# ScalarE's order in the first attention sequence: scalings behind the next block's exponentials

## The chip, the core and the metric

The kernel runs on one core of a Trainium2 chip. The metric is device time in microseconds (us). Three runs of the kernel before took 1680.72 to 1680.81 us, median 1680.8. One profiled execution gives the trace that is read here.

## The reference

Causal attention with a learned position bias, then a dense mixture of experts. All inputs and outputs are fp32.

```python
B, H, S, D = 4, 8, 576, 64          # attention
scores = q @ k.T / sqrt(D)
cum = cumsum(maximum(s, 0))
scores = where(causal, -1e9, scores + minimum(-(cum_i - cum_j), 0))
attn = exp(scores - max(scores)); attn = attn / (sum(attn) + 1e-9)
x = (attn @ v) as [2304, 512]        # N tokens, D_model

P = exp(x @ w_gate - max)            # 8 experts
for _ in range(8):                   # balance rows and columns
    P /= P.sum(1) + 1e-9; P /= P.sum(0) + 1e-9; P *= N / E
out = sum over e of P[:, e] * (relu(x @ w1[e]) @ w2[e])     # F = 1024
```

## The kernel before, in words

Each fp32 operand of a large product is split into a high and a low part, and three products of parts stand for one. Later stages use a scheme with seven products in place of eight for each 2x2 group of blocks. Those stages take most of the span and are not touched here.

The attention is done per head pair. There are 16 pairs, four per sequence; the first sequence is pairs 0 to 3, called pair 1 to pair 4 in this text. A pair has 576 query rows in five blocks of 128, 128, 128, 128 and 64 rows. Because of the causal mask block i needs only (i + 1) * 128 key columns, so the blocks have 128, 256, 384, 512 and 576 columns. The first four blocks are done for two heads each, on two score banks; in the fifth both heads share one tile of 128 rows, and it is computed in two halves of 288 columns. A block is named by its columns below. One block passes through these steps:

- TensorE computes the scores (tile sc, L605 in the first sequence, L587 later) in a ring of three PSUM banks.
- VectorE forms the row minimum (tile mn, L617) of the negated, masked scores and writes them to an SBUF tile T. There are seven T buffers.
- ScalarE takes the exponential (L652) in place and adds up each row (tile sm).
- VectorE adds 1e-9 to the sums (L703) and takes their reciprocal (tile rec, L709).
- ScalarE multiplies the tile by the reciprocal (L712): the scaling.
- TensorE transposes the tile (tr, L721), VectorE copies the transposes to SBUF (at, L726; for the fifth block al, L729 and L732), and TensorE multiplies them with v (pv, L751). ScalarE and VectorE take the high and low part of that as x (xh, L767 and L768).

Beside this GpSimd prepares the operands of later pairs (L492 to L503 and L556 to L563: casts and subtractions) and, with ScalarE, splits expert weights (L110, L111). A stream of matmuls of the first expert (L149, L178) and of the gate (L776) is given out between the attention blocks as x becomes ready, so TensorE has other work from the second half of the first sequence on.

The loop over the 80 blocks writes down, for step ti, the scores to exponentials of block ti, the sums to scaling of block ti - 1 (st1), the products with v of block ti - 3 and the transposes of block ti - 2. This is the order of the program text. The order on each engine is then set by a scheduler which takes a ready instruction for an engine that its own timeline has free, in program order where several are ready. `tc.issue_after(x)` adds that an instruction stands behind x. Once the order is fixed, each engine works through its own list strictly in turn.

Of the kernel before, what the change touches and what calls it, by code (L numbers as in the profile page):

```python
# [10 lines left out]
AF = mybir.ActivationFunctionType  # L11
# [34 lines left out]
def fused_kernel(ctx: ExitStack, tc: tile.TileContext, qT, kT, v, s, w_gate, wu, out):  # L46
    nc = tc.nc
# [282 lines left out]
    NP0 = 4  # L330
# [327 lines left out]
    last_exp = [None]  # L658
# [34 lines left out]
    def heads(t):  # L693
        return range(2 if t[1] < 4 else 1)

    def st1(t):

        g, i = t
        sm = sums.pop(t)
        nh = len(heads(t))  # L700
        n = (i + 1) * P if i < 4 else S
        if g < NP0:
            nc.vector.tensor_scalar_add(sm[:, :nh], sm[:, :nh], 1e-9)  # L703
        else:
            nc.scalar.activation(
                sm[:, :nh], sm[:, :nh], AF.Identity, bias=guard[:, 0:1], scale=1.0
            )
        rec = apool.tile([P, 2], F32, name="rec", tag="rec", bufs=2)
        nc.vector.reciprocal(out=rec[:, :nh], in_=sm[:, :nh])  # L709
        for j in heads(t):  # L710
            T = Ts[t, j][:, :n]
            nc.scalar.activation(T, T, AF.Copy, scale=rec[:, j : j + 1])  # L712

    def st2(t, j):

# [152 lines left out]
    for ti in range(NS + 3):  # L868
        if ti < NS:
            g, i = slots[ti]  # L870
# [7 lines left out]
        if 1 <= ti <= NS:  # L878
            st1(slots[ti - 1])
# [677 lines left out]
```

## Time and profile before

| | |
|---|---|
| runs (3), median | 1680.8 us (1680.72 to 1680.81) |
| profiled execution | 1679.26 us |
| its span | 1677.5 us, so 1.76 us lie around it |
| TensorE (PE) busy | 1657.0 us, 99% of the span |
| VectorE (DVE) busy | 1171.5 us, 70% |
| ScalarE (ACT) busy | 827.7 us, 49% |
| GpSimd (POOL) busy | 870.0 us, 52% |

Busy times count an engine as busy from the start to the end of an instruction; instructions of one engine overlap by up to a tenth of a microsecond where they follow each other. The idle time that a row gives in brackets is that of the engine just before the instruction, with the instruction that ended it. The clock in the view of stages is the one granted to TensorE, as a share of the full 2.4 GHz.

### The profile page before, as it was taken

The numbers are of one execution on the slowest core, as the hardware profiler recorded it, in microseconds if no ns is written. First come the engines' busy times: TensorE is split into PE (matmuls) and PEld (weight loads), VectorE is DVE, ScalarE is ACT, GpSimd is POOL, SyncE is SP. The second block draws the span as 40 slices with busy tenths as digits, with TensorE's granted clock in tenths as the row PEclk, the third lists the DMA queues.
The fourth block names the chain that finished last, engine by engine and source line by source line (L and its number), as shares of the span: only waits on it lengthen the run. The fifth ranks groups of instructions, "written<-read, shape, count | busy, mean of one in ns | idle before, by whom it ended". The sixth has DMA issues, their size and how long they took to land.

```text
span 1677.5 us, 31297 instructions
## 1 busy us (share of the span) xinstructions
PE 1657.0 (99%) x11213; PEld 1560.9 (93%) x11213; DVE 1171.5 (70%) x2310; ACT 827.7 (49%) x1792; POOL 870.0 (52%) x822
## 2 busy tenths in 40 slices
PE   8999999999999999999999999999999999999999
PEld 6798988888899999999899999999999999999998
DVE  7667666665776776676457777777777777777666
ACT  6777667434544444444235444444445444444443
POOL 7757877433554454454214554545554555455444
PEclk9999999999999999999999999999999999999999
DMA  7647766294975866875956566665688656566552
GB/s 208 176 131 230 212 186 186 92 354 136 316 241 198 276 235 200 279 240 185 354 176 204 182 193 186 187 187 177 204 305 260 193 186 191 182 192 186 187 184 89
DMA packets 202731, 347.54 MB, mean 207 GB/s; under 512 B 20592, under 2 KB 102512, under 8 KB 202512
## 3 DMA queue, kind: packets, MB, share of 16 engines
q1 hardware_dynamic: 202416, 345.23, 64.1%
q8 instruction: 89, 1.46, 0.3%
q14 instruction: 66, 0.54, 0.1%
q10 hardware_dynamic: 160, 0.31, 0.0%
HBM read 246.53 MB, written 94.96 MB: 204 GB/s over the span
## 4 chain that ended last, share of the span: by engine, by line
PE 91%; DVE 4%; ACT 2%; issue 1%; DMA 1%; POOL 0%; SPq 0%; ACTq 0%; DVEq 0%; POOLq 0%
PE c L1193 34%; PE zz L1314 13%; PE zz L1371 13%; PE y L1371 10%; PE g L149 4%; PE g L178 4%; PE sc L587 3%; PE pv L751 2%; PE tr L721 2%; PE c L149 2%; PE c L178 1%; DVE s L1168 1%; ACT T L712 1%; ACT T L652 1%; DVE h L253 1%
## 5 line engine op out<-in xcount | busy, mean ns | idle before, releaser
L253 POOL TENSOR_TENSOR w2o<-r,w2o 128x512 fp32r<-128x512 f32 x192 | 276.5, 1461 | 279.7 <-ACT w2o L1351 271.1
L1371 PE MATMUL zz<-w2o,h 128*128 128x256 f32 x2016 | 272.9, 280 | 0.0
L1193 PE MATMUL c<-xS,w1o 128*128 128x384 f32 x1344 | 271.6, 336 | 1.0 <-ACT t L1208 0.6
L1371 PEld LDWEIGHTS zz<-w2o,h 128*128 128x128 f32 x2016 | 263.3, 188 | 0.3 <-DVE h L253 0.2
L1314 PE MATMUL zz<-w2p,h 128*128 128x512 f32 x1008 | 256.8, 391 | 0.4 <-ACT h L1156 0.4
L1157 DVE SCALAR_TENSOR_TENSOR h<-z,h 128x384 fp32r<-128x384 f32 x252 | 192.7, 770 | 66.2 <-ACT h L1156 63.5
L1156 ACT ACTIVATE h<-z 128x384 fp32r<-128x384 f32 x252 | 130.6, 525 | 207.4 <-DVE z L256 203.5
L1193 PEld LDWEIGHTS c<-xS,w1o 128*128 128x128 f32 x1344 | 227.4, 188 | 2.5 <-DVE z L256 1.2
L1168 DVE SCALAR_TENSOR_TENSOR s<-z,s 128x384 f32<-128x384 f32 x224 | 182.0, 850 | 65.4 <-ACT s L1231 62.4
L253 POOL TENSOR_TENSOR h<-s,h 128x384 fp32r<-128x384 f32 x112 | 137.7, 1237 | 163.2 <-ACT h L1164 162.5
L1314 PEld LDWEIGHTS zz<-w2p,h 128*128 128x128 f32 x1008 | 186.9, 188 | 29.5 <-ACT h L1156 0.7
L1193 PE MATMUL c<-x,w1o 128*128 128x384 f32 x1008 | 203.0, 336 | 0.0
L1371 PE MATMUL y<-w2o,h 128*128 128x256 f32 x1512 | 201.6, 280 | 0.4 <-DVE a L1297 0.3
L1371 PEld LDWEIGHTS y<-w2o,h 128*128 128x128 f32 x1512 | 194.6, 188 | 1.0 <-DVE a L1297 0.5
L256 DVE TENSOR_TENSOR z<-c,t 128x384 f32<-128x384 f32 x252 | 136.7, 550 | 69.8 <-PE c L1193 65.0
L1193 PEld LDWEIGHTS c<-x,w1o 128*128 128x128 f32 x1008 | 170.5, 188 | 0.6
L1297 DVE SCALAR_TENSOR_TENSOR a<-zz,prob,a 128x256 f32<-128x256 f32 (+1 forms) x210 | 110.6, 530 | 67.6 <-PE zz L1371 52.9
L1164 ACT CAST h<-s 128x384 fp32r<-128x384 f32 x224 | 111.0, 513 | 75.7 <-DVE s L1168 70.7
L1193 PE MATMUL c<-xS,wp 128*128 128x384 f32 x672 | 134.5, 336 | 1.3 <-DVE z L256 1.3
L1193 PEld LDWEIGHTS c<-xS,wp 128*128 128x128 f32 x672 | 119.0, 188 | 9.6 <-DVE z L256 2.6
L1351 ACT CAST w2o<-r 128x1024 fp32r<-128x1024 f32 x98 | 102.5, 1047 | 50.9 <-PE y L1371 38.2
L253 POOL TENSOR_TENSOR wp<-s,wp 128x512 fp32r<-128x512 f32 x56 | 80.1, 1430 | 82.8 <-ACT wp L1083 69.7
(166 smaller groups left out, 2638.7 us busy)
## 6 DMA issues: line engine op xcount, KB each, us to landing
w1o<-w1d SPq DMA_DIRECT2D x392, 256.0 KB
w1d<-wp SPq DMA_DIRECT2D x84, 512.0 KB
r<-wu SPq DMA_DIRECT2D x70, 512.0 KB
r<-w2d SPq DMA_DIRECT2D x56, 512.0 KB
sa<-wu SPq DMA_DIRECT2D x28, 512.0 KB
w2d<-sb SPq DMA_DIRECT2D x56, 256.0 KB
wraw<-wu SPq DMA_DIRECT2D x20, 512.0 KB
xS<-xd_S SPq DMA_DIRECT2D x12, 768.0 KB
```

The costliest lines, as they stand in the source:

```text
L149: nc.tensor.matmul(ps[:, :n], lhsT=w1[:, w, o : o + P], rhs=xcols(b, x, k, n0, n), start=(k == 0 and t == 0), stop=(k == KD - 1 and t == 2),)
L253: (eng or nc.gpsimd).tensor_tensor(out=out, in0=a, in1=b, op=ALU.subtract)
L256: (eng or nc.gpsimd).tensor_tensor(out=out, in0=a, in1=b, op=ALU.add)
L1156: mark["a"] = nc.scalar.activation(t[:, 0], z, AF.Relu)
L1157: mark["v"] = nc.vector.scalar_tensor_tensor(out=t[:, 1], in0=z, scalar=0.0, in1=t[:, 0].bitcast(F32), op0=ALU.max, op1=ALU.subtract,)
L1164: nc.scalar.copy(t[:, 0], z)
L1168: nc.vector.scalar_tensor_tensor(out=out, in0=z, scalar=0.0, in1=other, op0=ALU.max, op1=op)
L1193: mm = nc.tensor.matmul(ps, lhsT=w[:, wl, k], rhs=x[:, xl, k], start=(fresh and k == 0 and t == 0), stop=(k == 1 and t == 2), skip_group_c ...
L1297: nc.vector.scalar_tensor_tensor(out=a, in0=ps, scalar=prob[:, c, e : e + 1], in1=a, op0=ALU.mult, op1=ALU.add)
L1314: mm = nc.tensor.matmul(zb[ci], lhsT=h[:, a, ci * P : (ci + 1) * P], rhs=w[:, b_], start=(ui == 0 and f == 0 and t == 0), stop=(ui == UPE ...
L1351: nc.scalar.copy(w[:, :, 0], r)
L1371: nc.tensor.matmul(ps, lhsT=h[:, a, ci * P : (ci + 1) * P], rhs=w[:, ui, b_], start=(fresh and ui == 0 and t == 0), stop=(ui == UPE - 1 an ...
```

## The change

In the first sequence (g below NP0 = 4, the first four pairs) each scaling is issued behind `last_exp[0]`, the last exponential written down so far. When step ti writes the scalings of block ti - 1, that is the last exponential of block ti. Outside the first sequence the line is as before. The three new lines shift what follows, so L712 before is L715 after.

```diff
         for j in heads(t):
             T = Ts[t, j][:, :n]
-            nc.scalar.activation(T, T, AF.Copy, scale=rec[:, j : j + 1])
+            with ExitStack() as st:
+                if g < NP0:
+                    st.enter_context(tc.issue_after(last_exp[0].ins))
+                nc.scalar.activation(T, T, AF.Copy, scale=rec[:, j : j + 1])
```

The first place is ScalarE's list at the start of pair 1, up to the first block of pair 2. L652 is the exponential of a block, L712 its scaling, and x2 stands for two heads. Before:

```order
L652 ACTIVATE T,sm<-T,mn 128x128 x2
L712 ACTIVATE T<-T,rec 128x128 x2
L652 ACTIVATE T,sm<-T,mn 128x256 x2
L712 ACTIVATE T<-T,rec 128x256 x2
L652 ACTIVATE T,sm<-T,mn 128x384 x2
L712 ACTIVATE T<-T,rec 128x384 x2
L652 ACTIVATE T,sm<-T,mn 128x512 x2
L712 ACTIVATE T<-T,rec 128x512 x2
L652 ACTIVATE T,sm<-T,mn 128x576
L767 CAST xh<-pv 128x256
L712 ACTIVATE T<-T,rec 128x576
L652 ACTIVATE T,sm<-T,mn 128x128 x2
```

And the same place now:

```order
L652 ACTIVATE T,sm<-T,mn 128x128 x2
L652 ACTIVATE T,sm<-T,mn 128x256 x2
L715 ACTIVATE T<-T,rec 128x128 x2
L652 ACTIVATE T,sm<-T,mn 128x384 x2
L715 ACTIVATE T<-T,rec 128x256 x2
L652 ACTIVATE T,sm<-T,mn 128x512 x2
L715 ACTIVATE T<-T,rec 128x384 x2
L652 ACTIVATE T,sm<-T,mn 128x576
L715 ACTIVATE T<-T,rec 128x512 x2
L770 CAST xh<-pv 128x256
L652 ACTIVATE T,sm<-T,mn 128x128 x2
L715 ACTIVATE T<-T,rec 128x576
```

Each scaling has moved behind the next block's exponentials. VectorE's list up to the first half of the 576 block is the same before and after.

The second place is VectorE's list from the end of pair 1 to the 256 block of pair 2. L617 is a row minimum (in two rows, the second reads out the minimum), L726 a copy of transposes. Before:

```order
L726 COPY at<-tr 128x384 x2
L703 TENSOR_SCALAR sm<-sm 128x1
L768 TENSOR_TENSOR xh<-pv,xh 128x256
L709 RECIPROCAL rec<-sm 128x1
L617 ISA T,mn<-sc,mask 128x128
L617 ISA mn 128x1
L617 ISA T,mn<-sc,mask 128x128
L617 ISA mn 128x1
L726 COPY at<-tr 128x512 x2
L617 ISA T,mn<-sc,mask 128x256
```

And now:

```order
L703 TENSOR_SCALAR sm<-sm 128x1
L729 COPY at<-tr 128x384
L709 RECIPROCAL rec<-sm 128x1
L729 COPY at<-tr 128x384
L617 ISA T,mn<-sc,mask 128x128
L617 ISA mn 128x1
L617 ISA T,mn<-sc,mask 128x128
L617 ISA mn 128x1
L771 TENSOR_TENSOR xh<-pv,xh 128x256
L729 COPY at<-tr 128x512 x2
L703 TENSOR_SCALAR sm<-sm 128x2
L617 ISA T,mn<-sc,mask 128x256
```

The lone addition of the 576 block has moved ahead of the 384 copies, and the addition of pair 2's first block ahead of the 256 minimum.

The third place is VectorE's list in pair 4, around the minima of the 384 block. Before:

```order
L768 TENSOR_TENSOR xh<-pv,xh 128x256
L703 TENSOR_SCALAR sm<-sm 128x2
L617 ISA T,mn<-sc,mask 128x384
L617 ISA mn 128x1
L617 ISA T,mn<-sc,mask 128x384
L617 ISA mn 128x1
L709 RECIPROCAL rec<-sm 128x2
L729 COPY al<-tr 128x512
```

And now:

```order
L617 ISA T,mn<-sc,mask 128x384
L617 ISA mn 128x1
L617 ISA T,mn<-sc,mask 128x384
L617 ISA mn 128x1
L732 COPY al<-tr 128x512
L703 TENSOR_SCALAR sm<-sm 128x2
L735 COPY al<-tr 128x128
L709 RECIPROCAL rec<-sm 128x2
```

The addition of the 256 block stood ahead of the 384 minima and now stands behind them and behind a copy.

## Rows read from the trace of the kernel before

**Rows 1.** Busy time by stage: stretch and length; busy time and instructions by engine; clock, DMA.
```profile
10.26:17.19 6.93, 4.08 (x31) 2.93 (x32) 4.07 (x19) 4.66 (x16) 5.87 (x11) 0.97 0.91 259
17.19:24.79 7.60, 6.97 (x55) 5.24 (x53) 6.34 (x24) 6.31 (x16) 5.07 (x9) 0.80 0.72 215
24.79:37.87 13.08, 12.16 (x131) 9.31 (x130) 9.88 (x43) 10.58 (x32) 6.87 (x9) 1.00 0.88 235
37.87:50.22 12.35, 11.52 (x119) 8.75 (x121) 9.16 (x41) 10.63 (x31) 9.86 (x19) 1.00 0.54 162
50.22:61.79 11.57, 9.32 (x102) 6.97 (x103) 10.09 (x31) 9.55 (x27) 10.93 (x15) 1.00 0.57 158
...
80.00:260.00 180.00, 180.00 (x1500) 161.17 (x1499) 119.94 (x389) 126.95 (x360) 132.77 (x178) 1.00 0.66 194
```

**Rows 2.** Waits, 10 to 62 us: who waited for whom, total, times, longest.
```profile
DVE sm L703 <- ACT T L652: 9.1, 10, 1.6
...
PE sc L605 <- DVE mn L617: 4.8, 5, 1.9
```

**Rows 3.** Timeline of ScalarE, pair 1: start, length, instruction, shapes, count, idle before.
```profile
11.66 0.69 ACT L712 ACTIVATE T<-T,rec 128x128 f32<-128x128 f32 x2 [0.52 <-DVE rec L709]
12.26 0.49 ACT L652 ACTIVATE T<-T,mn 128x256 f32<-128x256 f32 x1
...
15.57 0.60 ACT L652 ACTIVATE T<-T,mn 128x384 f32<-128x384 f32 x1
```

**Rows 4.** Timeline of VectorE, pair 1.
```profile
11.48 0.40 DVE L617 CUSTOM_DVE_ANT_0 T<-sc,mask 128x256 f32<-128x256 f32 x1
...
13.37 1.10 DVE L703 TENSOR_SCALAR sm<-sm 128x2 f32<-128x2 f32 x1 [1.13 <-ACT T L652]
...
14.58 0.54 DVE L617 CUSTOM_DVE_ANT_0 T<-sc,mask 128x384 f32<-128x384 f32 x1
...
16.90 0.17 DVE L703 TENSOR_SCALAR sm<-sm 128x2 f32<-128x2 f32 x1 [0.89 <-ACT T L652]
...
17.19 0.67 DVE L617 CUSTOM_DVE_ANT_0 T<-sc,mask 128x512 f32<-128x512 f32 x1
...
19.93 0.17 DVE L703 TENSOR_SCALAR sm<-sm 128x2 f32<-128x2 f32 x1 [0.41 <-ACT T L652]
```

**Rows 5.** All additions of L703: duration in ns, least, median, most.
```profile
L703 DVE TENSOR_SCALAR sm<-sm x20: 144/169/1211, 11.2 to 63.2; 128x2 f32<-128x2 f32 x16, 128x1 f32<-128x1 f32 x4
```

**Rows 6.** Timeline of GpSimd, pair 1.
```profile
13.18 1.92 POOL L497 TENSOR_TENSOR ops<-rawq,ops 128x512 fp32r<-128x512 f32 x3
15.18 1.43 POOL L503 TENSOR_TENSOR ops<-rawk,ops 128x576 fp32r<-128x576 f32 x1
...
19.45 1.08 POOL L494 CAST ops<-rawq 128x512 fp32r<-128x512 f32 x3
20.61 1.95 POOL L497 TENSOR_TENSOR ops<-rawq,ops 128x512 fp32r<-128x512 f32 x3
```

**Rows 7.** Timeline of TensorE, the scores of pair 1's 512 block.
```profile
15.18 2.02 PE L605 MATMUL sc<-ops 64*128 64x512 f32 x12 [1.90 <-DVE mn L617]
```

**Rows 8.** Timeline of VectorE, from pair 1 to pair 2.
```profile
23.59 1.28 DVE L726 COPY at<-tr 128x512 f32<-128x512 f32 x2
24.79 0.41 DVE L617 CUSTOM_DVE_ANT_0 T<-sc,mask 128x256 f32<-128x256 f32 x1
```

**Rows 9.** Timeline of VectorE, pair 2.
```profile
29.32 0.37 DVE L703 TENSOR_SCALAR sm<-sm 128x2 f32<-128x2 f32 x1 [1.61 <-ACT T L652]
```

**Rows 10.** Timeline of GpSimd, one subtraction in pair 2, one in pair 4.
```profile
28.38 1.28 POOL L111 TENSOR_TENSOR w<-wraw,w 128x512 fp32r<-128x512 f32 x1
...
53.08 1.41 POOL L559 TENSOR_TENSOR ops<-rx,ops 64x576 fp32r<-64x576 f32 x1
```

**Rows 11.** Timeline of VectorE, pair 4.
```profile
53.30 1.21 DVE L703 TENSOR_SCALAR sm<-sm 128x2 f32<-128x2 f32 x1
54.42 0.54 DVE L617 CUSTOM_DVE_ANT_0 T<-sc,mask 128x384 f32<-128x384 f32 x1
```

## The prediction

> **What bounds the kernel now.** I read the busy time of each engine by stage first [rows 1]. From 80 to 260 us TensorE is busy for all 180.00 us: there the span can only follow TensorE. The first sequence is different. I cut it where VectorE starts the row minima of a head pair's 256-column block: 24.79, 37.87, 50.22, and at 61.79 the last block of the fourth pair. In the five stretches up to there TensorE is busy 4.08 of 6.93, 6.97 of 7.60, 12.16 of 13.08, 11.52 of 12.35 and 9.32 of 11.57 us, so it idles 2.85 + 0.63 + 0.92 + 0.83 + 2.25 = 7.48 us. That idle time is all that the change can win, because the matmuls stay the same and what follows is packed. No other engine is full either: VectorE idles 11.99 of the five stretches' 51.53 us, ScalarE 9.80.
>
> The view of waits says why [rows 2]. VectorE's addition of 1e-9 to the sums (sm, L703) waits 9.1 us for ScalarE's exponential, and TensorE's scores wait 4.8 us for VectorE's row minimum, since a score bank is free only when the minimum has read it. So the three engines hand one block round in a ring: scores, minimum, exponential, sum and reciprocal, scaling, transposes.
>
> **The change part by part.** Nothing is added or removed: 36 scalings (four pairs, each with 4 blocks of two heads and one block of one) go behind the next block's exponentials. No DMA moves on ScalarE's queue; SyncE's list is shuffled by a few places, and its loads have tens of microseconds in hand. In the ring the scaling stood between two exponentials; now the exponential waits only for its own minimum, and the scaling runs while VectorE makes that.
>
> *Pair 1, worked through.* ScalarE has done the first block's exponentials at 11.14 and then idles 0.52 us for the reciprocal before the scalings of 11.66 [rows 3]; the 256 exponentials start behind these, at 12.26. The 256-column minimum of head 0 starts at 11.48 [rows 4] and takes 0.40, so in the new order they can start at about 11.93. The addition behind them starts at 13.37, so they took some 1.07; now they end at about 13.00, and the addition can start at 13.03.
>
> That 0.34 us may be worth more. The addition lasted 1.10 us at 13.37 and only 0.17 at 16.90 [rows 4]; the median of all 20 is 0.169, the longest 1.211 [rows 5]. GpSimd's three subtractions run from 13.18 for 1.92 us, and the first, of 512 columns, is the long one [rows 6]: the addition started inside it and ended, at 14.47, about with it. All six long additions of the sequence lie so. The one at 19.93 took 0.17 although GpSimd was casting (19.45 to 20.53): there a cast held nothing. An addition at 13.03 is ahead of 13.18, so it should take 0.17: the reciprocal and then the 384-column minimum start at about 13.32 instead of 14.58, the scores of block 4 at 13.92 instead of 15.18 [rows 7], and TensorE's wait of 1.90 shrinks by about 1.2.
>
> The next addition loses this. The 384 exponentials now start with their minimum, at about 13.89, and take the 1.30 that lie between 15.57 [rows 3] and the end that the addition of 16.90 waits for [rows 4]: that addition now comes at 15.22. GpSimd's next subtraction runs from 15.18 for 1.43 [rows 6], so I take the addition as held until 16.63, and the 512 minimum starts at 16.74 instead of 17.19: 0.45 is left. The margin is 0.04 us, so this is open (below).
>
> The Trainium skill, "SBUF — State Buffer", section "Who interferes with whom", says that VectorE and GpSimd share a port pair and that whoever issues first has it for the whole instruction, tensor_scalar being one of the kinds that take it. The rows agree for subtractions (a hold of 0.93 at 13.37) and not for casts. By that rule alone, with casts holding too, the cast block from 12.02 would also catch the addition at 13.03, pair 1 would gain nothing, and the sum below would be 1.46.
>
> From the 512 minimum to the next pair's 256 minimum took 17.19 to 24.79, 7.60 us, with VectorE busy for 6.34 [rows 1, 8]. In the new order one more addition stands in front of that minimum, the copy pair of 1.28 us (23.59) still does, and the lone addition of the 576 block comes near 20.8, inside the subtractions that begin at 20.61 [rows 6]. I take 7.7 us. So of 0.45 stay 0.34: the 256 minimum of pair 2 at 24.45. This is the main reason why I expect little: VectorE's copies fill what ScalarE gives up.
>
> *Pair 2.* VectorE idled 1.61 us up to 29.32 for the 384 exponentials, which stood behind the scalings of two blocks, and was then held 0.37 by the subtraction that began at 28.38 [rows 9, 10]. With these scalings moved, the exponentials start right behind their minimum; with the 0.34 carried on I put that at 26.9 and their end, 1.30 later, at 28.2, just ahead of 28.38. The upper end is the idle time and the hold less a normal addition, 1.61 + 0.20 = 1.81; the lower is nothing, where the subtraction wins and the addition ends at 29.69 as now. Also, the exponential of the 576 block now stands behind two scalings. I take a third, 0.63, nearer to the lower end, because that is what the row itself shows.
>
> *Pairs 3 and 4.* In pair 3 the copies stand ahead of the minima in the new order as in pair 2; bounds -0.8 to +0.83 (its TensorE idle time, and as much lost), and I take 0. In pair 4 the addition of 53.30 was held 1.21 us, and the 384 minima stood behind it, at 54.42 [rows 11]; TensorE's scores waited for them. In the new order both minima stand ahead of that addition. This frees at most 54.42 - 53.30 = 1.12; the hold now delays a scaling, which has slack. I take three quarters, 0.83, as later additions can be caught again; bounds -1.4 to 1.12.
>
> *Sum.* 0.34 + 0.63 + 0 + 0.83 = 1.80 us earlier at the end of the sequence, or 24% of the idle 7.48. Behind it the engines' lists are reshuffled on TensorE up to about its thousandth instruction of 10706 and on GpSimd and SyncE somewhat longer, then they agree; TensorE stays packed there, so the 1.80 should pass through. Scalings and transposes that come later are covered by the three other blocks in flight (seven T buffers); if that cover failed it would cost a scaling pair per block, 0.69 for the smallest [rows 3]. The profiled execution took 1679.26 (span 1677.5 and 1.76 around it), 1.54 below the median of 1680.8. Against its own time this gives 1677.46; against the median 1679.0.
>
> **The rivals.**
>
> *A, the additions slip ahead of GpSimd.* If the addition at 15.22 gets in before the subtraction, pair 1 gains 16.63 - 15.39 = 1.24 more, TensorE's granted clock, 0.80 on average from 17.19 to 24.79 after the idle stretch, need not fall, and pair 4 can recover 1.8 of its 2.25 idle. Sum 0.34 + 1.24 + 0.63 + 1.8 = 4.0: 1676.8. For it: the margin is 0.04 us and ScalarE's chain is truly shorter. Against it: VectorE's full list behind it.
>
> *B, VectorE takes the bound.* It is busy in 6.34 of 7.60 us from 17.19 on and in 10.09 of 11.57 in pair 4; the copies and holds eat what ScalarE gives. Then the only gain is about 0.3: 1680.5.
>
> *C, more holds: slower.* The change moves every addition against GpSimd's subtractions, and in pair 4 GpSimd is busy for 10.93 of 11.57 us [rows 1]. One newly caught addition costs up to 1.28 (the subtraction at 28.38) or 1.41 (the one at 53.08) [rows 10]. Three more that each wait in full, one in pair 2 and two in pair 4, cost 1.28 + 1.41 + 1.41 = 4.10, less the 1.80: 2.3 slower, 1683.1. It decides from 1.8 us of new holds on. Against it: six of 20 are held already, and moving an addition can free it as well.
>
> That the change doesn't do what it says is no rival: ScalarE's list shows the swap from the first block on. Only the last block of pair 4 has nothing to wait for but its own exponential.
>
> **How the numbers follow.** Forecast (gain 1.8, its own range 1677.6 to 1680.4): 0.40. A: 0.22. B: 0.23. C: 0.15. A measurement of this kernel tells about 0.2%, 3.4 us, from no change. Faster than 1677.4 is most of A and the edge of the forecast: 0.24. Slower than 1684.2 is half of C: 0.08. Within: 0.68. The range takes A and most of C in: 1675.7 to 1682.8.
>
> **What would show it.** In the changed profile: exponentials of the 256 block at about 11.9; the addition behind them 0.17 long; the third addition held by the subtraction of 15.18; the 256 minimum of pair 2 near 24.45, of pair 3 near 36.9; the 384 minima of pair 4 more than 1 us earlier against that pair's start; TensorE's idle time over the first 62 us down by about 1.8; and TensorE full from 80 us on. I am wrong if the long additions sum to much more or less than now, if TensorE is idle behind 80 us, or if the 256 minimum of pair 2 comes before 23.5.

## The result, and the profile after

The changed kernel takes 1689.9 us (median of 6 runs, 1688.9 to 1693.7) where the kernel before, run beside it, takes 1681.2 (1680.7 to 1682.6). The ratio is 1.0054, with a 95% interval of 1.0043 to 1.0065. So it is 8.7 us slower, where I had forecast 1.8 us faster, and it lies above the range. The profiled execution took 1690.09 us with a span of 1688.3. TensorE is busy for 1661.9 us of it (before: 1657.0) and so idles 26.4 us (before: 20.5). The 4.9 and the 5.9 add up to the 10.8 by which the span grew. The matmuls are the same ones and the mean granted clock fell from 0.999 to 0.995, so I put the 4.9 down to matmuls at a lower clock.

The view of stages says where. The columns are those of [rows 1]: stretch and length, busy time and instructions of TensorE, its weight loads, VectorE, ScalarE and GpSimd, then clock and DMA. This is after; it begins with the stretches of [rows 1]:

```profile
10.26:17.19 6.93, 5.29 (x31) 3.70 (x32) 4.78 (x19) 4.50 (x16) 5.88 (x11) 0.76 0.92 264
17.19:24.79 7.60, 6.04 (x58) 4.71 (x58) 6.63 (x29) 6.63 (x17) 5.06 (x9) 0.99 0.71 202
24.79:37.87 13.08, 12.29 (x134) 9.81 (x134) 10.78 (x43) 10.29 (x31) 6.27 (x8) 1.00 0.84 223
37.87:50.22 12.35, 10.76 (x121) 8.29 (x120) 10.05 (x41) 9.99 (x29) 10.46 (x20) 1.00 0.59 183
50.22:61.79 11.57, 7.95 (x92) 6.41 (x90) 10.37 (x23) 8.84 (x26) 11.34 (x16) 1.00 0.70 197
61.79:80.00 18.21, 16.13 (x126) 14.14 (x127) 12.26 (x44) 11.20 (x36) 5.02 (x7) 0.72 0.40 118
...
160.00:200.00 40.00, 35.74 (x292) 30.57 (x292) 24.04 (x71) 23.02 (x65) 27.13 (x38) 0.96 0.64 191
```

and the same view of before, for the two stretches that [rows 1] did not hold:

```profile
61.79:80.00 18.21, 16.77 (x151) 13.71 (x152) 10.51 (x41) 11.01 (x37) 9.17 (x14) 1.00 0.66 189
...
160.00:200.00 40.00, 40.00 (x331) 35.56 (x331) 24.92 (x81) 29.56 (x83) 35.67 (x52) 1.00 0.71 211
```

Two parts lose. From 50 to 80 us TensorE idles and then works at a granted clock of 0.72; from 160 to 200 us, where it had no gap at all, it idles 4.26 us.

**Up to 57 us TensorE gets ahead as forecast, though not term by term.** VectorE after, the starts of pairs 1 to 4, against [rows 1, 4, 8, 11]:

```profile
13.06 0.17 DVE L703 TENSOR_SCALAR sm<-sm 128x2 f32<-128x2 f32 x1 [0.82 <-ACT T L652]
...
13.35 0.54 DVE L617 CUSTOM_DVE_ANT_0 T<-sc,mask 128x384 f32<-128x384 f32 x1
...
15.27 1.37 DVE L703 TENSOR_SCALAR sm<-sm 128x2 f32<-128x2 f32 x1 [0.50 <-ACT T L652]
...
16.76 0.67 DVE L617 CUSTOM_DVE_ANT_0 T<-sc,mask 128x512 f32<-128x512 f32 x1
...
24.07 0.42 DVE L617 CUSTOM_DVE_ANT_0 T<-sc,mask 128x256 f32<-128x256 f32 x1
...
36.70 0.72 DVE L703 TENSOR_SCALAR sm<-sm 128x2 f32<-128x2 f32 x1
37.34 0.41 DVE L617 CUSTOM_DVE_ANT_0 T<-sc,mask 128x256 f32<-128x256 f32 x1
...
49.71 0.42 DVE L617 CUSTOM_DVE_ANT_0 T<-sc,mask 128x256 f32<-128x256 f32 x1 [0.64 <-PE sc L605]
...
52.14 0.55 DVE L617 CUSTOM_DVE_ANT_0 T<-sc,mask 128x384 f32<-128x384 f32 x1
```

I had put the addition at 13.03 and unheld, the 384 minimum at 13.32, the next addition at 15.22 and held, the 512 minimum at 16.74, pair 2 at 24.45. The 256 minima of pairs 2, 3 and 4 start 0.72, 0.53 and 0.51 us earlier than before, where the terms added up to 0.34, 0.97 and 0.97. So pair 1 gave twice its term, and pair 2 lost 0.19 in place of gaining 0.63: the minimum of 37.34 stands behind the addition of 36.70, which was held. The 384 minima of pair 4 start at 52.14 (before: 54.42), a gain of 1.77 within that pair, where its term was 0.83. The product with v of pair 3's last block starts at 54.77, where before it stood at 56.99: TensorE is 2.2 us ahead.

**Then one addition stands still for 5 us.** VectorE after, pair 4's 512 block, and what GpSimd does meanwhile:

```profile
57.83 5.06 DVE L703 TENSOR_SCALAR sm<-sm 128x2 f32<-128x2 f32 x1 [1.20 <-ACT T L652]
```

```profile
57.34 1.41 POOL L559 TENSOR_TENSOR ops<-rx,ops 64x576 fp32r<-64x576 f32 x1
58.71 1.25 POOL L111 TENSOR_TENSOR w<-wraw,w 128x512 fp32r<-128x512 f32 x1
59.91 0.14 POOL L542 MEMSET ops<- 128x64 f32 x1
...
60.26 0.65 POOL L556 CAST ops<-rawq 128x576 fp32r<-128x576 f32 x1
60.86 0.66 POOL L557 CAST ops<-rawk 128x576 fp32r<-128x576 f32 x1
61.48 0.78 POOL L556 CAST ops<-rawq 128x512 fp32r<-128x512 f32 x2
62.21 0.66 POOL L557 CAST ops<-rawk 128x576 fp32r<-128x576 f32 x1
62.95 1.40 POOL L563 TENSOR_TENSOR ops<-rawq,ops 64x576 fp32r<-64x576 f32 x1
```

Every GpSimd instruction starts some 0.03 to 0.06 us before the last one ends, until the cast of 62.21 ends at 62.87 and the next starts at 62.95. The addition ends in that gap, at 62.89; it met one GpSimd instruction and stood through ten more. The copies that TensorE waits for stand behind it on VectorE, so TensorE has nothing to do, and its clock falls:

```profile
57.95 0.22 PE L587 MATMUL sc<-ops 128*128 128x128 f32 x1
63.43 0.66 PE L724 MATMUL tr<-ident,T 128*128 128x128 f32 x2 [5.26 <-DVE at L729]
```

In stretches of two microseconds the granted clock is 1.00 up to 60, then 0.92, and 0.50 from 62 to 70: 1.2 in place of 2.4 GHz. All additions of L703 after, against [rows 5]:

```profile
L703 DVE TENSOR_SCALAR sm<-sm x20: 144/256/5061, 11.0 to 65.8; 128x2 f32<-128x2 f32 x16, 128x1 f32<-128x1 f32 x4
```

**The second loss** ends in two waits of TensorE:

```profile
169.64 0.50 PE L587 MATMUL sc<-ops 128*128 128x256 f32 x2 [2.80 <-DVE mn L617]
...
197.07 0.74 PE L587 MATMUL sc<-ops 128*128 128x256 f32 x4 [0.71 <-DVE mn L617]
```

That minimum stood on VectorE behind a cast of head operands (L557), which waited for its load in the first case and was held by GpSimd in the second:

```profile
168.49 0.60 DVE L557 CAST ops<-rawk 128x576 fp32r<-128x576 f32 x1 [4.55 <-DMA rawk<-kT]
...
192.62 3.96 DVE L557 CAST ops<-rawk 128x576 fp32r<-128x576 f32 x1
```

Why the load is late stands in SyncE's list. First before, then after; the columns are start, length, instruction and count:

```profile
152.48 0.59 SPq L96 DMA_DIRECT2D xd<-xh  x1
153.17 1.21 SPq L363 DMA_DIRECT2D rawk<-kT  x2
154.47 1.22 SPq L363 DMA_DIRECT2D rawq<-qT  x2
155.78 1.19 SPq L363 DMA_DIRECT2D rawk<-kT  x2
```

```profile
158.72 0.59 SPq L96 DMA_DIRECT2D xd<-xh  x1
159.41 1.21 SPq L363 DMA_DIRECT2D rawk<-kT  x2
161.91 0.56 SPq L268 DMA_DIRECT2D sx<-xd  x1
162.56 2.18 SPq L363 DMA_DIRECT2D rawq<-qT  x2
164.83 1.19 SPq L363 DMA_DIRECT2D rawk<-kT  x2
```

After, a load of x for the next stage (L268) has come in front of the next head's loads. It reads what the store of 158.72 (L96) writes, so the whole queue stands from 160.62 to 161.91 until that has landed. The last loads start 9.05 us later than before, while TensorE was 4.4 us late (product with v of the pair at hand: 155.59 before, 159.95 after). Of the 9.05 the queue had 6.24 already when that store started (158.72 against 152.48); the other 2.81 come behind it. Why it was 6.24 late and not 4.4 stays open.

### The profile page after: what moved, and what is told of

The parts are those of the page before. It is cut to its first block, busy times and chain, and to the rows that moved or that the text cites. A ratio compares the mean times of both kernels' runs of the same rounds, so it can differ in the third digit from the quotient of the medians.

```text
span 1688.3 us, 31292 instructions
## 1 busy us (share of the span) xinstructions
PE 1661.9 (98%) x11213; PEld 1566.0 (93%) x11213; DVE 1180.6 (70%) x2310; ACT 826.4 (49%) x1792; POOL 871.1 (52%) x822
## 4 chain that ended last, share of the span: by engine, by line
PE 89%; DVE 4%; POOL 2%; issue 1%; DMA 1%; ACT 1%; SPq 1%; ACTq 0%; DVEq 0%; POOLq 0%
PE c L1196 34%; PE zz L1317 13%; PE zz L1374 13%; PE y L1374 10%; PE g L149 4%; PE g L178 4%; PE sc L587 2%; PE pv L754 2%; PE tr L724 2%; PE c L149 2%; PE c L178 1%; DVE s L1171 1%; DMA wraw<-wu 1%; DVE h L253 1%; DVE T L617 0%
```

## The experiments

Three theories stood at the start. H: the held addition and what it hands on is all of the loss. H+Q: the hold is one cause, SyncE's reordered list a second. S: the later scalings are at fault, and the hold fills a time that would be idle anyway. Seven kernels were run. Gains are given by the third column, the median less that of the kernel before, run beside it. "Lost to the clock" is the mean span times one minus the mean granted clock, both over all runs of the row (6 to 29): the work that TensorE would have done in that time at the full clock. "Rest" is the mean span without it. The record gives a run's clock to three digits, and one unit of the third is 1.7 us of the span; by the scatter of the runs both columns are uncertain by some half a microsecond.

| kernel | median us | less before beside it | ratio to before, interval | mean span | lost to the clock | rest |
|---|---|---|---|---|---|---|
| before (beside 1 to 4) | 1681.0 | | | 1679.4 | 4.6 | 1674.8 |
| after | 1689.9 | +8.7 | 1.0054 (1.0043 to 1.0065) | 1688.5 | 10.4 | 1678.1 |
| 1: after, other addition | 1681.0 | 0.0 | 0.9998 (0.9989 to 1.0008) | 1679.7 | 5.7 | 1673.9 |
| 2: after, loads first | 1686.5 | +5.4 | 1.0031 (1.0020 to 1.0043) | 1684.0 | 8.4 | 1675.6 |
| 3: after, both | 1676.9 | -4.2 | 0.9977 (0.9967 to 0.9987) | 1675.2 | 4.0 | 1671.3 |
| 4: after, pair 4 split | 1684.6 | +3.6 | 1.0015 (1.0006 to 1.0025) | 1682.2 | 6.6 | 1675.7 |
| 5: before, other addition | 1676.0 | -5.4 | 0.9971 (0.9960 to 0.9981) | 1674.4 | 2.2 | 1672.2 |
| 6: before, loads first | 1681.7 | +0.3 | 1.0005 (0.9996 to 1.0014) | 1680.1 | 4.0 | 1676.1 |
| 7: after, no addition, loads first | 1678.6 | -2.7 | 0.9983 (0.9973 to 0.9992) | 1676.4 | 4.7 | 1671.6 |

**1. Another instruction for the addition.**

```diff
-            nc.vector.tensor_scalar_add(sm[:, :nh], sm[:, :nh], 1e-9)
+            nc.vector.tensor_reduce(
+                out=sm[:, :nh], in_=sm[:, :nh].unsqueeze(2), axis=AX.X, op=ALU.add
+            )
```

> The changed kernel with one thing replaced: the addition of 1e-9 to the sums (line 703, first sequence, 20 instructions of VectorE) becomes a sum over an axis of length 1, so the 1e-9 is left out; every engine's list is otherwise that of the changed kernel, instruction for instruction. Theory H (the hold is the cause, all of it): VectorE's addition for pair 4's last block was held 5.06 us behind GpSimd, and the 11 us follow from that one wait, the half-speed matmuls behind it and the lateness that it hands on. Then no instruction of that line is held, the gap on TensorE at 58 to 63 us and the half clock after it go, and the time is 1677 to 1680 us. Theory H+Q (two causes): the hold costs what is lost up to 93 us, some 4 to 6 us counted from where the kernel stood just before, and the second loss at 158 to 200 us comes from SyncE's reordered list, in which a load that waits for a store to land stands ahead of the loads of heads; then it is 1682 to 1686 us, and TensorE still idles some 4 us between 160 and 200 us. Theory S (the rival: the later scalings are themselves the cause, the hold only fills an idle time that was there anyway): 1688 to 1691 us.

It is 8.7 us faster than the changed kernel, and S falls. No instruction of the line is held any more; one of them starts at 55.83, inside the subtraction of 55.53:

```profile
L703 DVE TENSOR_REDUCE sm<-sm x20: 143/154/156, 11.0 to 59.0; 128x2 f32<-128x2 f32 x16, 128x1 f32<-128x1 f32 x4
```

```profile
55.83 0.15 DVE L703 TENSOR_REDUCE sm<-sm 128x2 f32<-128x2 f32 x1 [1.70 <-ACT T L652]
```

```profile
55.53 1.40 POOL L559 TENSOR_TENSOR ops<-rx,ops 64x576 fp32r<-64x576 f32 x1
```

The Trainium skill, "SBUF — State Buffer", section "Who interferes with whom", says that a tensor_reduce never contends with GpSimd on trn2; these 20 rows agree. The second loss is still there, which speaks for H+Q against H, though 1681.0 lies 1 us under the 1682 to 1686 of H+Q and 1 above the range of H, and TensorE idles 2.5 us between 160 and 200 us where H+Q said some 4:

```profile
161.36 0.73 PE L587 MATMUL sc<-ops 128*128 128x256 f32 x2 [2.21 <-DVE mn L617]
```

**2. The head loads first.** In the loads of x (L268):

```diff
                 for i, o in enumerate(XRAW):
-                    nc.sync.dma_start(out=xs[a][:, i], in_=xd[p, o][:, :, k, ts])
+                    with ExitStack() as st:
+                        if (p, a, o) == (0, 3, "22"):
+                            st.enter_context(tc.issue_after(heads_in[0].ins))
+                        nc.sync.dma_start(out=xs[a][:, i], in_=xd[p, o][:, :, k, ts])
```

> The changed kernel with one edge more: of the stage loads sx<-xd (line 268) one, the fourth job's block 22, is ordered behind the head loads before it, so that on SyncE's list the next head's four loads (rawq, rawk) stand ahead of that load, which waits for a store to land. TensorE, VectorE and ScalarE keep their lists; some GpSimd work moves too. Theory H: the head loads had slack that the first loss used up, the second loss stays at least in part, 1687 to 1690 us. Theory H+Q: the gaps of TensorE between 165 and 175 us (some 3.2 us) and the half-speed matmuls around them go, and the time is 1684 to 1687 us, with the 5.06 us hold still there. Theory S: as before this edit, 1688 to 1691 us.

3.3 us faster than the changed kernel, and in the range of H+Q. Below, lines behind the edit count three on. The queue no longer stands, and TensorE's wait shrinks from 2.80 to 1.17; that of 0.71 near 197 us is gone, because GpSimd's list changed there too and the cast is no longer held. So the gain is not that of the loads' order alone. The 5.06 us hold is still there, now 5.07.

```profile
159.29 1.21 SPq L366 DMA_DIRECT2D rawk<-kT  x2
160.59 1.19 SPq L366 DMA_DIRECT2D rawq<-qT  x2
161.87 2.14 SPq L366 DMA_DIRECT2D rawk<-kT  x2
```

```profile
167.65 0.50 PE L590 MATMUL sc<-ops 128*128 128x256 f32 x2 [1.17 <-DVE mn L620]
```

**3. Both edits.**

> Both edits: no addition on line 703 that GpSimd can hold (the 1e-9 left out), and the head loads ahead of the waiting stage load. Theory H: the same as the first edit alone, 1677 to 1680 us. Theory H+Q: 3 to 5 us faster than the first edit alone, 1677 to 1680 us. Theory S: 1685 to 1691 us.

4.2 us faster than the first edit alone and 12.9 faster than the changed kernel; the two gains apart are 8.7 and 3.3. H predicted no difference between 1 and 3 and falls. The two gains add up within the noise of a microsecond. Of the second loss this wait is the longest that is left:

```profile
159.80 0.50 PE L590 MATMUL sc<-ops 128*128 128x256 f32 x2 [0.67 <-DVE mn L620]
```

**4. Only pair 4's additions in another form.**

```diff
-            nc.vector.tensor_scalar_add(sm[:, :nh], sm[:, :nh], 1e-9)
+            for j in ([slice(0, nh)] if g < 3 else [slice(j, j + 1) for j in range(nh)]):
+                nc.vector.tensor_scalar_add(sm[:, j], sm[:, j], 1e-9)
```

> The changed kernel, but only pair 4's additions are split, each 128x2 addition into two of 128x1 (nothing is left out; pairs 1 to 3 keep theirs; the lists are otherwise the same). In the trace no 128x1 addition of that line was ever held. Theory H and H+Q, if the form of the instruction decides whether it is held: as the first edit, 1677 to 1680 us by H, 1682 to 1686 us by H+Q. If instead any addition that comes at that moment is held, the 5 us wait at 58 us is back in one of the halves, and the time stays at 1688 to 1691 us. Theory S: 1688 to 1691 us.

5.1 us faster than the changed kernel, in the range of H+Q. None of pair 4's nine additions is held, though eight of them start inside a subtraction of GpSimd. That of 57.46 lies in the middle of one:

```profile
57.46 0.15 DVE L704 TENSOR_SCALAR sm<-sm 128x1 f32<-128x1 f32 x1 [0.55 <-ACT T L652]
```

```profile
56.91 1.29 POOL L111 TENSOR_TENSOR w<-wraw,w 128x512 fp32r<-128x512 f32 x1
```

So by the medians 5.1 of the 8.7 us are pair 4's and 3.6 those of the ordinary holds in pairs 1 to 3 (by the mean spans 6.3 and 2.5). Here the form of the same addition decides whether it is held at all.

**5. The first edit in the kernel before** (the same diff).

> The kernel before with the same replacement as the first experiment (the additions of line 703 of the first sequence as a sum over an axis of length 1, the 1e-9 left out; all lists otherwise those of the kernel before). It tells how much of the 4.2 us by which both edits together are below the kernel before (1676.9 against 1681.0) comes from the additions alone, and how much from the later scalings. By the lengthened additions in the trace of before (1.10, 0.37, 0.88, 1.21, 0.76 and 0.35 us, six, against 0.17 unheld) at most 3.6 us can come back, and only what lies on the path. Theory A (the later scalings are worth what the prediction said, 1.8 us, once nothing is held): 1678.5 to 1679.5 us. Theory B (the later scalings are worth nothing, all of the 4.2 us is the additions'): 1676.5 to 1677.5 us. Theory C (before, the holds lie beside other waits): 1680.5 to 1681.5 us, and then the later scalings alone are worth some 4 us.

This I had not expected: 1676.0 us, below all three ranges, and nearest to B. The held additions of the kernel before cost it 5.4 us, more than the 3.65 by which its six long ones exceed 0.17, and no stretch of this profiled execution has a clock below 1.00. But those six are one sample. The two profiled executions are 3.3 us apart (1679.26 and 1675.98), which the 3.65 cover. In the profiled execution of experiment 6, where VectorE's list is that of before, and GpSimd's too up to 200 us, eight additions are long (0.35, 1.10, 0.68, 1.16, 1.22, 1.21, 0.75 and 0.36 us), 5.5 us above 0.17 in all. So what is held changes from one execution to the next. Against experiment 3 the moved scalings show no gain: 1676.0 without them and 1676.9 with them, and the two intervals to before overlap widely.

**6. The second edit in the kernel before** (the same diff).

> The kernel before with the one edge of the second experiment (the fourth job's load of block 22 behind the head loads before it); TensorE, VectorE and ScalarE keep their lists. If the edge only repairs what the change's reordering of SyncE's list broke, it does nothing here: TensorE has no idle time between 160 and 200 us in the trace of before, 1680 to 1682 us. If loads in that order are worth something in any kernel: 1676 to 1679 us.

1681.7 against 1681.3 beside it: nothing. The edge only mends what the change's new order broke.

**7. No addition.** The 20 additions go; the rest as in 3.

```diff
-        if g < NP0:
-            nc.vector.tensor_scalar_add(sm[:, :nh], sm[:, :nh], 1e-9)
-        else:
+        if g >= NP0:
```

> The changed kernel with the edge of the second experiment and without the 20 additions at all in the first sequence (the 1e-9 is left out: each sum holds an exponential of 0, so it is at least 1, and 1e-9 is below half a unit in the last place of a float32 there). Against both edits together it saves some 0.15 us of VectorE and one instruction between the exponential and the reciprocal, 20 times. If VectorE or that chain bounded the first sequence, it would be 1 to 3 us below 1676.9 us; if not, 1676 to 1678 us.

1678.6, 0.6 above both ranges and not faster than 3. So neither VectorE's time for these additions nor the one step in the chain costs anything that these runs resolve. It loses 4.7 us to the clock where 3 loses 4.0, and the rest is equal within 0.4; both are inside the scatter.

## Why the prediction was wrong

The sum of the experiments first, each against the kernel before beside it. With no addition held, the change costs 0.0 + 5.4 = 5.4 us (experiments 1 and 5). Of these the second edit takes back 0.0 + 4.2 = 4.2 (1 and 3), and 1.2 are left (3 and 5), which the intervals do not tell from nothing. The other 8.7 - 5.4 = 3.3 us are longer holds: held additions cost 5.4 us before and 8.7 after.

The profiled executions say where. Each row gives the start, in us, of the products with v of a pair's last block (pv<-al, 20 matmuls), for pair 3 and for three later pairs:

| kernel | pair 3 | pair at 155 us | the next | next but one |
|---|---|---|---|---|
| before | 56.99 | 155.59 | 174.85 | 196.57 |
| after | 54.77 | 159.95 | 184.41 | 207.86 |
| 1: after, other addition | 52.75 | 152.25 | 175.58 | 199.06 |
| 3: after, both | 52.73 | 152.23 | 173.11 | 194.84 |
| 5: before, other addition | 53.79 | 152.20 | 171.87 | 193.59 |

Up to 155 us the holds make the difference: after is 4.4 us late there, and 1, 3 and 5 are 3.3 to 3.4 early. Behind it 1 loses 5.8 us, 3 loses 1.6 and 5 loses 0.4. From 1 to 3 the second edit wins 2.5 us by the third product and 1.8 more by the fourth; in between, a cast of head operands stands for 3.97 us in 1 (183.79), and none there for more than 0.84 in 3. So of its 4.2 us some 2.5 belong to the loads and 1.8 to that cast, as far as one execution of each can tell. The 1.2 by which 3 stays behind 5 arise there too (1.6 against 0.4).

Two steps failed: the price of a hold (3.3 us more than before), and SyncE's loads, which I put at nothing (4.2 us with what hangs on them). The 1.80 that should have come off for the scalings did not reach the end.

*The moved scalings.* The mechanism was right: the exponentials come sooner, and TensorE is 2.2 us ahead at 57 us, where the terms of pairs 1 to 3 gave 0.97 and all four 1.80. That the sum came near is partly luck, because pair 2's term failed and those of pairs 1 and 4 came out double. With nothing held, the scalings alone are worth 1.06 us at pair 3 (3 against 5 in the table), and at 152 us nothing. Why that goes is not shown. The clock is one candidate. Pair 1 in the profiled executions of experiments 5, 3 and 6:

```profile
10.26:17.19 6.93, 4.69 (x37) 3.33 (x38) 4.06 (x20) 5.48 (x18) 5.87 (x11) 1.00 0.90 249
```

```profile
10.26:17.19 6.93, 5.99 (x30) 4.12 (x31) 4.10 (x21) 4.77 (x17) 5.87 (x11) 0.57 0.93 257
```

```profile
10.26:17.19 6.93, 4.87 (x26) 2.98 (x26) 4.07 (x18) 4.50 (x16) 5.87 (x11) 0.61 0.89 245
```

In 3 TensorE is busy for longer than in 5 and does less, 30 instructions against 37, at a clock of 0.57. But 6, which lacks the change, has 0.61 there, so these rows do not tie the low clock to the change. In the means of the table experiment 3 has 0.9 us less rest than experiment 5 and loses 1.8 us more to the clock; no run took the clock away to prove it.

*The price of a hold* is the first step that failed. Rival C had the mechanism, its place in pair 4, and a turning point of 1.8 us of new holds. The long additions exceed 0.17 us by 3.65 us in all before and by 9.4 after, so that 5.7 are new. But I priced a hold at no more than one GpSimd instruction, 1.41 us, because all six of before had ended with one. The one of 57.83 lasted through eleven. By the rows that I had, pair 4's GpSimd was busy for 10.93 of 11.57 us [rows 1]; that was the only bound in sight, and I did not use it. The range was said to take most of C in, but it ended at 1682.8, below C's own 1683.1.

*"A cast holds nothing"* rested on one row and was wrong. That row of [rows 6] is three casts in one. The first of them is

```profile
19.45 0.61 POOL L494 CAST ops<-rawq 128x512 fp32r<-128x512 f32 x1
```

so it ended at 20.06, and the addition of 19.93 at 20.10: a hold would not have shown. After, an addition that met such a cast with more of it still to run lasted 0.34 us and ended with it:

```profile
18.73 0.61 POOL L494 CAST ops<-rawq 128x512 fp32r<-128x512 f32 x1
```

```profile
19.03 0.34 DVE L703 TENSOR_SCALAR sm<-sm 128x2 f32<-128x2 f32 x1
```

The rule of the Trainium skill ("SBUF — State Buffer", section "Who interferes with whom") by which whoever issues first has the ports for the whole instruction was right on casts here. The estimate that pair 1 would then gain nothing did not come true, because the casts of 12.02 ran only to 13.10 and the addition came at 13.06. The rule gives one instruction as the length; the 5.06 us through eleven go beyond it, and there the measurement decides.

*SyncE's loads with tens of microseconds in hand* is the second step that failed. The last head loads started 9.05 us later with TensorE 4.4 us late, and TensorE then waited 2.80 us: they had less than 5 us in hand. I looked at how far the list was shuffled, not at which of its entries waits for a landing and what stands behind it. The second edit, which moves GpSimd's list as well, takes back 4.2 us, of which some 2.5 by the loads.

*TensorE packed from 80 us on, so the 1.80 passes through.* A packed engine passes a gain on only if those that feed it keep up, and it passes every loss on: from 200 us on a difference of 11 us stays to the end. And 1 and 3, which no addition holds up, lost 5.8 and 1.6 us between 155 and 197 us of what they had gained.

*The holds of before.* I took their cost as what the rows beside them freed. Experiment 5 says 5.4 us for the additions. The larger prize was in a line next to the one that was changed.

Of the tests that I named, the times of pair 1 were met. Pair 3's minimum came at 37.34 and not near 36.9, and TensorE's idle time over the five stretches rose from 7.48 to 9.20 us. Two of the three signs of being wrong came: longer additions in sum, and idle time behind 80 us.

## What to carry to other kernels

A short VectorE instruction that GpSimd can hold mostly waits for one GpSimd instruction, but the price of a bad case is bounded only by GpSimd's gapless run at that moment. If it stands on the path between engines, it is worth giving it a form that was not held: here that alone is worth 5.4 us in the kernel before, more than moving the work around it. (Experiments 1, 3 and 5 leave the 1e-9 out; the split of experiment 4 keeps it.) When an edit lets a scheduler reorder a DMA queue, look for an entry that waits for a landing and for the loads that now stand behind it. That a gain of idle time is worth less if TensorE's clock falls in the gaps that are left is likely from the traces, but not tested.

## What the runs showed of the hardware

A hold mostly ends with the GpSimd instruction that it met, even where the next one starts 0.02 to 0.06 us before that. In the profiled executions of before, after and experiments 2, 4 and 6, 39 additions lasted more than 0.2 us. Of these 24 met an instruction with such a successor and came through at the first boundary (one of them, in two traces, at the second, as it had begun only 0.03 us ahead of the first). The same goes for 20 casts of head operands on VectorE of more than 0.7 us, in before, after and experiments 1 to 4. At two places it was otherwise: the addition of 57.83 (5.06 us after, 5.07 in experiment 2) and the cast of 192.62 (3.96 us after, and 3.97 in experiments 1 and 4, where it comes at 183.79 and 186.93). As they come again in other kernels, it looks like a matter of the place and not of chance. The addition stood up to the first gap; the cast came through at the end of the fourth instruction, though the fifth had begun. Both met a subtraction of L559, but additions at 53.30 and 60.09 before met one too and came through at its end [rows 10, 11]. What tells these apart stays open; no run tried it.

An addition of 128x1 was not held in any of these traces (none lasted over 0.16 us), one of 128x2 often.
